# Windowed attention and an ELU layer on one core: half of the first q and k loaded through the GpSimd queue with a cast

## The chip, the cores and the metric

The kernel runs on one core of a Trainium2 chip. The metric is the time of one execution on the device in microseconds (us), the median of several runs; lower is better. A core has a matrix engine (TensorE, PE in the profile; its weight loads are shown apart as PEld), a vector engine (VectorE, DVE), an engine for functions (ScalarE, ACT), a general one (GpSimd, POOL) and one that mostly issues transfers (SyncE, SP). Each runs its instructions in the order of the program and waits on semaphores for the others. Transfers (DMAs) can be issued by SP, ACT and POOL; a DMA that changes the element type on its way is issued by POOL here.

## What is computed

First attention with a window of 32 positions to either side, for 8 batches of 8 heads, 576 positions and 64 channels; then a layer that takes the 4608 x 512 result to 2048 channels, applies ELU, and takes it back to 512. All inputs are float32 in memory.

```python
def _attn_ref(q, k, v):
    B, H, S, D = q.shape                       # 8, 8, 576, 64
    scores = np.matmul(q, k.transpose(0, 1, 3, 2)) / np.sqrt(D)
    pos = np.arange(S)
    mask = np.abs(pos[:, None] - pos[None, :]) <= 32
    scores = np.where(mask, scores, -1000000000.0)
    attn = np.exp(scores - np.max(scores, axis=-1, keepdims=True))
    attn = attn / (np.sum(attn, axis=-1, keepdims=True) + 1e-09)
    return np.matmul(attn, v)

def _moe_ref(x, w_in, w_out):                  # x: 4608 x 512
    h = x @ w_in                               # 512 x 2048
    g = np.where(h > 0.0, h, np.exp(np.minimum(h, 0.0)) - 1.0)
    return g @ w_out                           # 2048 x 512
```

## The kernel before

**Tiling.** A "pair" is two blocks of 64 query positions, 128 rows of the result; there are 36 pairs. A "token tile" is two pairs, 256 rows; there are 18. For a token tile the layer runs in 8 steps of 256 hidden channels each, so the main loop (L609) has 144 steps `kk`, and two more at its end. `mm1(kk)` multiplies the transposed tile `xT` with two 128-column pieces of `w_in` (8 matmuls of 256 columns) into the accumulator `ps`, in bank h0 or h1 by turns. ACT makes `e_sb = exp(ps)`, DVE makes `m_sb = e_sb - 1`, and `elu(kk)`, which is called one step later, makes `g_sb` from `ps` and `m_sb` on DVE. `mm2`, two steps later, multiplies `g_sb` with `w_out` (4 matmuls of 512 columns) into `psY`. The steps of the first two token tiles are woven together (L539 to L541): steps 0 to 3 belong to tile 0, steps 4 to 7 to tile 1, then the rest of both. Step 4 is thus the first that needs pairs 2 and 3.

**Attention of a pair.** `scores` (L281: 32 matmuls of 64 rows), `exponential` on ACT (L296), `mask` on DVE (L303), `pv` (L312: 32 matmuls with 64 weight columns, which write the two halves of the partitions by turns), `normalize` on DVE (L326: a reciprocal and a product), `x_transpose` (L337: four PE transposes) and `x_evac` (L353), which gives `xT`. Queries and keys are needed transposed, with channels on partitions (`qT`, `kT`); values stand in `V_e`, and, rotated by 64 positions, in `V_o` (`rotate_v`, L137, on DVE).

**How q and k come in.** For the first batches `load_qk` (L115) loads float32 to SBUF, in two DMAs (even and odd heads) of 288 KB each for half a batch; `cast_qk` (L236) makes bfloat16 of it; `transpose_qk` (L266) transposes nine 128 x 128 pieces per half batch on PE and evicts them with ACT or DVE. A half is 288 positions: `HALF_A` is the first, `HALF_B` the second. Later batches go through DRAM (`write_rows`, `transpose_rows`).

**How values and weights come in.** `load_v` (five blocks per batch, numbered 0 to 4), `load_w_in` and `load_w_out` (four chunks each of 1 MB float32) are issued by POOL and cast on the way. Chunk 0 serves steps 0, 1, 4 and 5, chunk 1 steps 2, 3, 6 and 7, chunk 2 steps 8 to 11, chunk 3 steps 12 to 15. POOL's order before is: values 1, 0, 2; three `affine_select` for the masks; w_in 0; values 3, 4; w_out 0; w_in 1; w_out 1; w_in 2; w_out 2; values 0, 1, 2 of the second batch; w_in 3; w_out 3; values 3, 4 of the second batch.

**What sets the order.** The schedule is written out by hand: each engine runs in the order in which the program emits. The front (L170 to L429) is straight code, with `idle` matmuls (L376) on zeros that fill PE's gaps. In the loop, `at(kk, slot, fn, ...)` hangs work on step `kk`: "dve" runs after `elu(kk-1)` and ahead of `mm1(kk)`, "mid" after `mm1(kk)`, "end" after `mm2`. A `gate` (L148) is a tiny DMA on SP that reads a piece of a tile; SP's later loads wait until what it reads is there. Before, `HALF_B` of the first batch follows a gate on the masks, `HALF_A` of the second a gate on w_in 1, and `HALF_B` of the second and the whole third batch a gate on w_in 3.

Of the kernel before, what the change touches and what calls it, by code (L numbers as in the profile page):

```python
# [21 lines left out]
def kernel(  # L22
# [9 lines left out]
    nc = tc.nc  # L32

    B, H, S, D = q.shape
    WIN = 32
# [5 lines left out]
    QB = 64  # L41
    NQB = S // QB
    NPAIR = B * NQB // 2
    HP = H // 2
    NC = 128 // HP
    SJ = S // NC
    VS = 5
# [13 lines left out]
    cpool = ctx.enter_context(tc.tile_pool(name="const", bufs=1))  # L61
# [50 lines left out]
    WHOLE, HALF_A, HALF_B = (0, SJ), (0, SJ // 2), (1, SJ // 2)  # L112
    qk_f = {}

    def load_qk(b, which, part, engs=(nc.sync, nc.sync)):  # L115
        z, nj = part
        t = lpool.tile([128, 2, nj * D], FP32, tag=f"f{which}{nj}",
                       name=f"f{which}")
        qk_f[b, which, z] = t
        src = (q, k)[which][b, :, z * NC * nj:(z + 1) * NC * nj, :].rearrange(  # L120
            "(g h) (c j) d -> c g h (j d)", h=2, j=nj)
        for h in range(2):
            engs[h].dma_start(out=t[:, h, :], in_=src[:, :, h, :])

    def load_v(b, m):
        lo = 128 * m - WIN
        p0 = max(0, -lo)
        p1 = min(128, S - lo)
        nc.gpsimd.dma_start(  # L129
            out=V_e[b % 3][p0:p1, m, :, 0:D],  # L130
            in_=v[b, :, lo + p0:lo + p1, :].rearrange("h p d -> p h d"))
# [5 lines left out]
    def rotate_v(b, m0, m1, parts=(0, 1)):  # L137
        e, o = V_e[b % 3], V_o[b % 3]
        for z in parts:
            nc.vector.tensor_copy(o[64 * z:64 * (z + 1), m0:m1],  # L140
                                  e[64 * (1 - z):64 * (2 - z),
                                    m0 + z:m1 + z])
# [17 lines left out]
    def load_w_out(c):  # L160
        n = NFO // 4
        nc.gpsimd.dma_start(
            out=w_out_sb[:, c * n:(c + 1) * n, :],
            in_=moe_w_out[c * n * 128:(c + 1) * n * 128, :].rearrange(
                "(o p) f -> p o f", p=128))

    def w_in_at(c):
        return w_in_sb[0:1, 0, (c + 1) * (D_FF // 4) - 1:(c + 1) * (D_FF // 4)]
# [7 lines left out]
    def edges(i):  # L176
        nc.vector.memset(V_e[i][:, :, :, D:VD], 1.0)
        nc.vector.memset(V_e[i][0:32, 0], 0.0)
        nc.vector.memset(V_e[i][96:128, VS - 1], 0.0)
        if i < 2:  # L180
            for c0, n in ((KPAD - WIN, HP), (KPAD + HP * S, 1)):
                z = kT[i][:, c0:c0 + WIN]
                nc.vector.memset(_bap(z, [z.ap[0], [S, n], [1, WIN]]), 0.0)

    edges(0)
    edges(1)

    ident = cpool.tile([128, 128], BF16)
    make_identity(nc, ident)

    masks = cpool.tile([128, 5, QB], BF16, name="masks")
    nc.gpsimd.memset(masks, 1.0)
    nc.gpsimd.affine_select(
        out=masks, in_=masks, compare_op=ALU.is_ge, fill=0.0,
# [3 lines left out]
        base=2 * WIN, pattern=[[0, 5], [1, QB]], channel_multiplier=-1)  # L200
    for m in (1, 0, 2):
        load_v(0, m)
    for mi in (0, 4):
        nc.gpsimd.affine_select(
            out=masks[:, mi, :], in_=masks[:, mi, :], compare_op=ALU.is_ge,
            fill=0.0, base=-WIN, pattern=[[0, QB]], channel_multiplier=1)
    nc.gpsimd.affine_select(
        out=masks[:, 3, :], in_=masks[:, 3, :], compare_op=ALU.is_ge,
        fill=0.0, base=128 - WIN - 1, pattern=[[0, QB]],
        channel_multiplier=-1)  # L210
    kinds = ["FE", "EE", "EL", "LF"]

    gate(masks[0:1, 3, 0:1])
    for which in range(2):
        load_qk(0, which, HALF_B)
    load_w_in(0)
    for m in (3, 4):
        load_v(0, m)
    load_w_out(0)
    load_w_in(1)  # L220
    load_w_out(1)

    def kind(jb):
        qb = jb % NQB
# [5 lines left out]
    def copy_on(eng, d_, s_):  # L230
        if eng is nc.scalar:
            nc.scalar.copy(d_, s_)  # L232
        else:
            eng.tensor_copy(d_, s_)  # L234
# [12 lines left out]
    def keys_or_queries(b, which):  # L247
        if which == 0:
            return qT[b % 2].rearrange("p g s -> p (g s)")
        return kT[b % 2][:, KPAD:KPAD + HP * S]  # L250
# [12 lines left out]
        nc.sync.dma_start_transpose(  # L263
            out=keys_or_queries(b, which), in_=in_dram.pop((b, which)))

    def transpose_qk(b, which, part, j0, n, evac, tag="t0"):  # L266
        z, nj = part
        src = qk_b[b, which, z]
        pt = ps_tile([128, 1024 if n <= 8 else 2048], BF16, tag, "ptx")
        for j in range(n):  # L270
            nc.tensor.transpose(  # L271
                pt[:, j * 128:(j + 1) * 128], src[:, j0 + j, :], ident)
        d = keys_or_queries(b, which)
        copy_on(evac,
                _bap(d, [d.ap[0], [S, HP], [nj, NC], [1, n]],
                     z * NC * nj + j0),
                _bap(pt, [pt.ap[0], [1, HP], [HP, NC], [128, n]]))

    st = {}

# [56 lines left out]
    def x_transpose(i):  # L337
        x_st, tag = st[i][3:]
        pt = ps_tile([128, NDO, 128], BF16, tag, "psXT")
        for do in range(NDO):  # L340
            nc.tensor.transpose(  # L341
                pt[:, do, :], x_st[:, 2 * do:2 * do + 2, :], ident)
        st[i] = pt
# [9 lines left out]
    def x_evac(i, eng=nc.vector):  # L353
        copy_on(eng, xT_of(i), st.pop(i))
# [12 lines left out]
    def front_cast(which, part, eng):  # L367
        for j0, n in SPLIT:
            cast_qk(0, which, part, j0, n, eng)

    def front_transpose(which, part, evac, tags):
        for (j0, n), tag in zip(SPLIT, tags):
            transpose_qk(0, which, part, j0, n, evac, tag)


    def idle(n, tag):  # L376
        ps = ps_tile([128, 512], FP32, tag, "ps_idle")
        for _ in range(n):
            nc.tensor.matmul(ps, lhsT=zeros[:, 0:128], rhs=zeros,
                             start=True, stop=True)  # L380

    warm = cpool.tile([128, 1], FP32)
    nc.scalar.activation(warm, zeros[:, 0:1], AX.Exp)

    idle(8, "y1")
    front_cast(0, HALF_A, nc.vector)
# [11 lines left out]
    for i in (0, 1):  # L398
        mask(i)
    pv(0)  # L400
    idle(2, "h0")
    pv(1)
    for i in (0, 1):
        normalize(i)
    for i in (0, 1):
        idle(1, "h1")
        x_transpose(i)
        x_evac(i, nc.scalar)
    idle(2, "h1")
    front_cast(0, HALF_B, nc.scalar)  # L410
    front_cast(1, HALF_B, nc.vector)


    load_w_in(2)
    load_w_out(2)
    for m in range(3):
# [2 lines left out]
    load_w_out(3)  # L419
    for m in range(3, VS):  # L420
        load_v(1, m)
    gate(w_in_at(1))
    for which in range(2):
        load_qk(1, which, HALF_A)
    gate(w_in_at(3))
    for which in range(2):
        load_qk(1, which, HALF_B)
# [8 lines left out]
    def at(kk, slot, fn, *args):  # L436
        tasks.setdefault((kk, slot), []).append((fn, args))
# [11 lines left out]
        at(kk + 2, "end", x_evac, i, nc.scalar)  # L449


    at(1, "mid", front_transpose, 1, HALF_B, nc.scalar, ("s", "u"))
    at(1, "mid", front_transpose, 0, HALF_B, nc.vector, ("y0", "y1"))
    at(2, "dve", rotate_v, 0, 2, VS - 1)
    for i, tag in ((2, "s"), (3, "u")):
        at(1, "mid", scores, i, tag)
        at(1, "mid", exponential, i)
        at(2, "dve", mask, i)
    at(2, "dve", lambda: mm2(1))
    for i in (2, 3):  # L460
        at(2, "dve", pv, i)
        at(2, "dve", normalize, i)
        at(3, "mid" if i == 3 else "dve", x_transpose, i)
        at(3, "mid" if i == 3 else "dve", x_evac, i, nc.scalar)
    at(4, "dve", swap_pools)

    for part, kq in ((HALF_A, 7), (HALF_B, 15)):
        for which in range(2):
            at(kq - 1 + which, "mid", cast_qk, 1, which, part, 0, SJ // 2,
               (nc.scalar, nc.vector)[which])  # L470
            at(kq + which, "mid", transpose_qk, 1, which, part, 0, SJ // 2,
               nc.scalar, "s")
    at(8, "dve", edges, 2)
    at(16, "dve", hold_v, 2)
    for m in range(VS):
        at(16 + m, "mid", load_v, 2, m)
# [132 lines left out]
    for kk in range(NSTEP + LAG):  # L609
        run(kk, "first")  # L610
        if 1 <= kk < NSTEP:
            elu(kk - 1)
        run(kk, "dve")
        if kk < NSTEP:
            mm1(kk)
        run(kk, "mid")

        for n in {1: (0,), 2: (), 3: ()}.get(
                kk, (kk - LAG,) if kk >= LAG else ()):
            mm2(n)  # L620
        run(kk, "end")
# [30 lines left out]
```

The softmax here doesn't subtract the row's maximum and nothing guards it: scores larger than these inputs give would overflow.

## Time and profile before

| what | before |
|---|---|
| median of 5 runs | 313.08 us (310.97 to 315.32) |
| the profiled execution | 312.87 us, of which the span of instructions is 311.1 us |
| granted clock of TensorE over the span | 0.998 |
| `mm1` of step 0 / 2 / 4 / 8 begins at | 15.20 / 24.09 / 27.40 / 35.03 us |
| `mm2` of step 0 begins at | 21.39 us |
| scores of pairs 2 and 3 begin at | 20.55 us |
| an `mm1` matmul, an `mm2` matmul | 273 ns, 379 ns each (pipelined: eight and four take about 0.87 us) |
| `exp` / `m_sb` / `g_sb` of one step | 595 / 435 / 686 ns |

Times within the profile count from the start of the span. In the page's second part the span is cut into 40 slices, and a digit is the busy share in tenths. In an answer in order of time a row gives start, duration, engine, line, operation, output and input, shape and count, and in brackets how long the engine was idle before it and what released it. A table of stretches gives, for each engine, busy us and count of instructions, then granted clock, DMA share and GB/s. The rows of the DMA queues give packets, MB and share of the 16 engines; the share can pass 100% since packets overlap.

### The profile page before, as it was taken

The page shows a single profiled execution, that of the slowest core. Times are in us where ns is not written, and L with a number is a line of the kernel's source. Part 1 is how long each engine was busy: PE and PEld are TensorE (multiplying, and loading weights), DVE is VectorE, ACT ScalarE, POOL GpSimd, SP SyncE. Part 2 cuts the span into 40 slices and gives each one's busy share as a digit, 9 for nine tenths or more (in the row PEclk, how much of TensorE's full clock was granted, in tenths as well). Part 3 has the DMA queues.
Part 4 walks back from the last instruction along what each step waited for, and adds up shares of the span by engine and source line. Part 5 has one row for each costly group of instructions (what it writes and reads, how often), then busy time and mean ns, then how long its engine had stood idle before and what let it go on. Part 6 is the DMA issues. An engine that isn't in the chain of part 4 may idle for free.

```text
span 311.1 us, 7510 instructions
## 1 busy us (share of the span) xinstructions
PE 292.9 (94%) x2996; PEld 197.5 (64%) x3048; DVE 247.3 (80%) x480; ACT 170.7 (55%) x256; POOL 44.0 (14%) x60
## 2 busy tenths in 40 slices
PE   7768999999999799999999999999999999999994
PEld 3446666676666466666666666666676666676662
DVE  6587688899979588888888888888888787876663
ACT  3564656787664575568366836673636363634331
POOL 8733000824210022020202010000000000000000
PEclk9999999999999999999999999999999999999999
DMA  9999999999999899999999999678111111111011
GB/s 191 230 204 240 221 235 367 323 209 228 276 111 134 263 246 227 217 175 291 276 139 174 217 300 158 190 167 172 70 36 67 36 70 35 70 34 70 0 70 68
DMA packets 91657, 52.93 MB, mean 170 GB/s; under 512 B 76518, under 2 KB 80614, under 8 KB 91622
## 3 DMA queue, kind: packets, MB, share of 16 engines
q1 hardware_dynamic: 48022, 36.77, 47.9%
q0 software_dynamic: 41728, 8.92, 39.9%
q10 hardware_dynamic: 1872, 6.75, 7.1%
q8 instruction: 24, 0.39, 0.6%
q14 instruction: 11, 0.09, 0.1%
HBM read 36.70 MB, written 15.34 MB: 167 GB/s over the span
## 4 chain that ended last, share of the span: by engine, by line
PE 77%; DMA 12%; DVE 4%; POOL 3%; issue 2%; ACT 1%; SPq 0%; DVEq 0%; POOLq 0%
PE ps L558 35%; PE psY L592 35%; DMA w_out_sb<-in_moe_w_out_dram 4%; DMA in_dram<-qkb 4%; PE psS L320 3%; DMA f<-in_k_dram 3%; PE psS L288 3%; DMA kT<-in_dram 2%; POOL Ve L129 1%; PE ptx L271 1%; DVE g_sb L577 1%; DVE pm L308 1%; PE psXT L341 1%; DVE m_sb L567 1%; DVE x_st L332 0%
## 5 line engine op out<-in xcount | busy, mean ns | idle before, releaser
L565 ACT ACTIVATE e_sb<-ps 128x512 f32<-128x512 f32 (+1 forms) x145 | 86.2, 595 | 121.5 <-PE ps L558 116.0
L558 PE MATMUL ps<-xT,w_in_sb 128*128 128x256 bf16 x1152 | 149.3, 273 | 1.8 <-ACT xT L232 1.2
L592 PE MATMUL psY<-w_out_sb,g_sb 128*128 128x512 bf16 x525 | 139.1, 379 | 3.3 <-issue 0.6
L558 PEld LDWEIGHTS <-w_in_sb 128*128 128x128 bf16 x1152 | 110.8, 98 | 40.3 <-issue 2.1
L577 DVE SCALAR_TENSOR_TENSOR g_sb<-ps,m_sb 128x512 bf16<-128x512 f32 (+1 forms) x145 | 99.5, 686 | 12.9 <-PE ps L558 0.5
L567 DVE TENSOR_SCALAR m_sb<-e_sb 128x512 bf16<-128x512 f32 (+1 forms) x145 | 63.0, 435 | 34.7 <-ACT e_sb L565 32.7
L592 PEld LDWEIGHTS <-g_sb 128*128 128x128 bf16 x576 | 54.6, 98 | 38.5 <-DMA w_out_sb<-in_moe_w_out_dram 0.3
L129 POOL DMA_DIRECT2D Ve<-in_v_dram x40 | 34.8, 881 | 133.2 <-PE psS L320 92.1
L299 ACT ACTIVATE pu<-psS 128x1024 bf16<-128x1024 f32 x36 | 36.5, 1019 | 3.6 <-PE psS L288 3.6
L232 ACT CAST qkb<-f 128x768 bf16<-128x768 f32 (+3 forms) x32 | 26.7, 838 | 0.0
L332 DVE TENSOR_TENSOR x_st<-psS,rc 128x512 bf16<-128x512 f32 x36 | 24.9, 692 | 1.2
L308 DVE TENSOR_TENSOR pm<-pu,masks 128x1024 bf16<-128x1024 bf16 x36 | 24.6, 683 | 1.6 <-ACT pu L299 1.6
L320 PEld LDWEIGHTS <-pm 128*64 128x64 bf16 x576 | 11.2, 110 | 10.4 <-DVE pm L308 7.2
L288 PE MATMUL psS<-qT,kT 64*128 64x64 bf16 x576 | 12.1, 191 | 4.6 <-DVE qT L234 2.1
L288 PEld LDWEIGHTS <-kT 64*128 64x128 bf16 x576 | 9.8, 95 | 9.4 <-issue 5.4
L320 PE MATMUL psS<-Ve,pm 128*64 128x65 bf16 x320 | 13.7, 196 | 0.9 <-DVE pm L308 0.7
L140 DVE COPY Vo<-Ve 64x1040 bf16<-64x1040 bf16 x32 | 13.7, 428 | 1.0
L234 DVE COPY y_sb<-psY 128x512 f32<-128x512 f32 x18 | 12.3, 686 | 1.0 <-PE psY L592 0.9
L320 PE MATMUL psS<-Vo,pm 128*64 128x65 bf16 x256 | 12.5, 197 | 0.2 <-DVE pm L308 0.2
L234 DVE CAST qkb<-f 128x1152 bf16<-128x1152 f32 (+3 forms) x14 | 8.8, 653 | 4.2 <-DMA f<-in_k_dram 3.8
L232 ACT COPY y_sb<-psY 128x512 f32<-128x512 f32 x18 | 10.5, 582 | 2.2 <-PE psY L592 2.2
L271 PE MATMUL ptx<-ident,qkb 128*128 128x128 bf16 x108 | 8.9, 235 | 1.4 <-DVE qkb L234 1.3
(32 smaller groups left out, 67.0 us busy)
## 6 DMA issues: line engine op xcount, KB each, us to landing
out_dram<-y_sb SPq DMA_DIRECT2D x35, 256.0 KB, 2.5
f<-in_q_dram SPq DMA_DIRECT2D x12, 576.0 KB, 8.9
f<-in_k_dram SPq DMA_DIRECT2D x12, 576.0 KB, 10.4
in_dram<-qkb ACTq DMA_DIRECT2D x10, 576.0 KB, 8.9
Ve<-in_v_dram POOLq DMA_DIRECT2D x24, 128.0 KB, 11.1
w_in_sb<-in_moe_w_in_dram POOLq DMA_DIRECT2D x4, 512.0 KB, 16.1
w_out_sb<-in_moe_w_out_dram POOLq DMA_DIRECT2D x4, 512.0 KB, 17.0
f<-in_q_dram SPq DMA_DIRECT2D x7, 288.0 KB, 6.2
```

Of the source, the lines that this page charges most:

```text
L129: nc.gpsimd.dma_start(out=V_e[b % 3][p0:p1, m, :, 0:D], in_=v[b, :, lo + p0:lo + p1, :].rearrange("h p d -> p h d"))
L232: nc.scalar.copy(d_, s_)
L288: nc.tensor.matmul(psS[:, h % 2, hp * 128 + z * QB:hp * 128 + (z + 1) * QB], lhsT=kT[b % 2][base:base + 64, KPAD + hp * S + QB * qb - WIN: ...
L299: nc.scalar.activation(pu, _bap(psS, [psS.ap[0], [1, 1024]]), AX.Exp, scale=SCALE)
L308: nc.vector.tensor_mul(pm, pu, _bap(mm, [mm.ap[0], [0, H], [1, 2 * QB]]))
L320: nc.tensor.matmul(psS[QB * z:QB * (z + 1), par, hp * VD:(hp + 1) * VD], lhsT=pm[:, par * HP + hp, z * QB:(z + 1) * QB], rhs=vv[:, qb // 2 ...
L332: nc.vector.tensor_mul(x_st, _bap(psS, [psS.ap[0], [VD, HP], [512, 2], [1, D]]), _bap(rc, [rc.ap[0], [2, HP], [1, 2], [0, D]]))
L558: nc.tensor.matmul(ps[:, j, :], lhsT=w_in_sb[:, do, fo * 128:(fo + 1) * 128], rhs=xT[t][:, :, do, :], start=(do == 0), stop=(do == NDO - 1))
L565: nc.scalar.activation(e_sb, ps, AX.Exp)
L567: nc.vector.tensor_scalar(m_sb, e_sb, -1.0, None, ALU.add)
L577: nc.vector.scalar_tensor_tensor(g_t[kk][:, z * w:(z + 1) * w, :], ps, 0.0, m_t[kk][z], ALU.max, ALU.min)
L592: nc.tensor.matmul(psY[t][ts], lhsT=g_sb[:, j, ts * 128:(ts + 1) * 128], rhs=w_out_sb[:, s * FG + j, :], start=(s == 0 and j == 0), stop=( ...
```

## The change

`load_cast` loads half a batch of q or k from POOL into a bfloat16 tile (one buffer for q, one for k), cast on the way, in two DMAs by even and odd heads. It is used for `HALF_B` of the first batch and `HALF_A` of the second; SP's loads of these, their two gates and their casts on ACT and DVE go. `transpose_qk` transposes such a tile by heads: two transposes of 64 columns, one for each half of the output's partitions, where there was one of 128.

POOL's order becomes: values 1, 0, 2; `HALF_B` of q and of k; w_in 0; the three `affine_select`; values 3, 4; w_out 0; w_in 1; w_out 1; `HALF_A` of q and of k of the second batch; w_in 2 and the rest as before.

In the front, the transposes of `HALF_B` of q stand between `pv(0)` and `pv(1)`, evicted by ACT, and those of k between the output transposes of pairs 0 and 1, evicted by DVE; most idle matmuls there go. `rotate_v` of the first batch's last two blocks is split: its part 0 stands ahead of the loop, its part 1 behind `mm1(0)`. Scores and exponentials of pairs 2 and 3 follow `mm1(0)`, ahead of `mm1(1)`; their products with the values follow `mm1(1)` and `mm2(0)`, where they followed `mm2(1)` in step 2. The memsets `edges(2)` move from step 8 to step 6. An option `later` of `transpose_qk` is added and not used.

```diff
+    def load_cast(b, which, part):
+        z, nj = part
+        t = cpool.tile([128, 2, nj * D], BF16, tag=f"c{which}",
+                       name=f"c{which}")
+        qk_c[b, which, z] = t
+        src = (q, k)[which][b, :, z * NC * nj:(z + 1) * NC * nj, :].rearrange(
+            "(g h) (c j) d -> c g h (j d)", h=2, j=nj)
+        for h in range(2):
+            nc.gpsimd.dma_start(out=t[:, h, :], in_=src[:, :, h, :])
...
-    gate(masks[0:1, 3, 0:1])
-    for which in range(2):
-        load_qk(0, which, HALF_B)
-    load_w_in(0)
-    for m in (3, 4):
-        load_v(0, m)
...
         for j in range(n):
-            nc.tensor.transpose(
-                pt[:, j * 128:(j + 1) * 128], src[:, j0 + j, :], ident)
+            if (b, which, z) in qk_c:
+                for h in range(2):
+                    nc.tensor.transpose(
+                        pt[64 * h:64 * (h + 1), j * 128:(j + 1) * 128],
+                        qk_c[b, which, z][:, h, (j0 + j) * D:
+                                          (j0 + j + 1) * D], ident)
...
+    for which in range(2):
+        load_cast(0, which, HALF_B)
+    load_w_in(0)
+    for mi in (0, 4):
+        nc.gpsimd.affine_select(
+            out=masks[:, mi, :], in_=masks[:, mi, :], compare_op=ALU.is_ge,
...
+    for m in (3, 4):
+        load_v(0, m)
+    load_w_out(0)
+    load_w_in(1)
+    load_w_out(1)
...
     pv(0)
-    idle(2, "h0")
+    front_transpose(0, HALF_B, nc.scalar, ("h0", "h1"))
     pv(1)
     for i in (0, 1):
         normalize(i)
-    for i in (0, 1):
-        idle(1, "h1")
-        x_transpose(i)
-        x_evac(i, nc.scalar)
+    x_transpose(0)
+    x_evac(0, nc.scalar)
+    front_transpose(1, HALF_B, nc.vector, ("y0", "y1"))
+    x_transpose(1)
+    x_evac(1, nc.scalar)
     idle(2, "h1")
-    front_cast(0, HALF_B, nc.scalar)
-    front_cast(1, HALF_B, nc.vector)
+    for which in range(2):
+        load_cast(1, which, HALF_A)
     load_w_in(2)
...
-    gate(w_in_at(1))
-    for which in range(2):
-        load_qk(1, which, HALF_A)
+    rotate_v(0, 2, VS - 1, (0,))
     gate(w_in_at(3))
...
-    at(1, "mid", front_transpose, 1, HALF_B, nc.scalar, ("s", "u"))
-    at(1, "mid", front_transpose, 0, HALF_B, nc.vector, ("y0", "y1"))
-    at(2, "dve", rotate_v, 0, 2, VS - 1)
-    for i, tag in ((2, "s"), (3, "u")):
-        at(1, "mid", scores, i, tag)
-        at(1, "mid", exponential, i)
-        at(2, "dve", mask, i)
+    at(0, "mid", rotate_v, 0, 2, VS - 1, (1,))
+    at(0, "mid", scores, 2, "s")
+    at(0, "mid", scores, 3, "u")
+    at(1, "mid", lambda: mm2(0))
+    for i in (2, 3):
+        at(0, "mid", exponential, i)
+        at(1, "dve", mask, i)
+        at(1, "mid", pv, i)
+    at(1, "mid", normalize, 2)
+    at(1, "end", x_transpose, 2)
+    at(1, "end", x_evac, 2, nc.scalar)
     at(2, "dve", lambda: mm2(1))
-    for i in (2, 3):
-        at(2, "dve", pv, i)
-        at(2, "dve", normalize, i)
-        at(3, "mid" if i == 3 else "dve", x_transpose, i)
-        at(3, "mid" if i == 3 else "dve", x_evac, i, nc.scalar)
+    at(2, "dve", normalize, 3)
+    at(2, "mid", x_transpose, 3)
+    at(2, "mid", x_evac, 3, nc.scalar)
...
-            at(kq - 1 + which, "mid", cast_qk, 1, which, part, 0, SJ // 2,
-               (nc.scalar, nc.vector)[which])
+            if part is HALF_B:
+                at(kq - 1 + which, "mid", cast_qk, 1, which, part, 0, SJ // 2,
+                   (nc.scalar, nc.vector)[which])
...
-    at(8, "dve", edges, 2)
+    at(6, "dve", edges, 2)
...
-        for n in {1: (0,), 2: (), 3: ()}.get(
+        for n in {2: (), 3: ()}.get(
```

More of the change, by code (lines that the diff above doesn't have):

```diff
@@ L123, in load_qk @@
             engs[h].dma_start(out=t[:, h, :], in_=src[:, :, h, :])
+    qk_c = {}
+    def load_cast(b, which, part):
[7 more added lines that the diff above has]
+            nc.gpsimd.dma_start(out=t[:, h, :], in_=src[:, :, h, :])
     def load_v(b, m):
@@ L183, in edges @@
                 nc.vector.memset(_bap(z, [z.ap[0], [S, n], [1, WIN]]), 0.0)
+    ident = cpool.tile([128, 128], BF16)
+    make_identity(nc, ident)
     edges(0)
     edges(1)
-    ident = cpool.tile([128, 128], BF16)
-    make_identity(nc, ident)
     masks = cpool.tile([128, 5, QB], BF16, name="masks")
@@ L202 @@
         load_v(0, m)
[L203 to L210, printed above, removed]
-    kinds = ["FE", "EE", "EL", "LF"]
-    gate(masks[0:1, 3, 0:1])
-    for which in range(2):
-        load_qk(0, which, HALF_B)
-    load_w_in(0)
-    for m in (3, 4):
-        load_v(0, m)
-    load_w_out(0)
-    load_w_in(1)
-    load_w_out(1)
+    kinds = ["FE", "EE", "EL", "LF"]
     def kind(jb):
@@ L264, in transpose_rows, with transpose_qk, evict @@
             out=keys_or_queries(b, which), in_=in_dram.pop((b, which)))
-    def transpose_qk(b, which, part, j0, n, evac, tag="t0"):
+    def transpose_qk(b, which, part, j0, n, evac, tag="t0", later=None):
         z, nj = part
-        src = qk_b[b, which, z]
         pt = ps_tile([128, 1024 if n <= 8 else 2048], BF16, tag, "ptx")
         for j in range(n):
-            nc.tensor.transpose(
-                pt[:, j * 128:(j + 1) * 128], src[:, j0 + j, :], ident)
[L273 to L277, printed above, removed]
+            if (b, which, z) in qk_c:
[4 more added lines that the diff above has]
+                                          (j0 + j + 1) * D], ident)
+            else:
+                nc.tensor.transpose(
+                    pt[:, j * 128:(j + 1) * 128],
+                    qk_b[b, which, z][:, j0 + j, :], ident)
+        def evict():
+            d = keys_or_queries(b, which)
+            copy_on(evac,
+                    _bap(d, [d.ap[0], [S, HP], [nj, NC], [1, n]],
+                         z * NC * nj + j0),
+                    _bap(pt, [pt.ap[0], [1, HP], [HP, NC], [128, n]]))
+        if later is None:
+            evict()
+        else:
+            later.append(evict)
     st = {}
@@ L369, in front_cast, with front_transpose @@
             cast_qk(0, which, part, j0, n, eng)
-    def front_transpose(which, part, evac, tags):
+    def front_transpose(which, part, evac, tags, later=None):
         for (j0, n), tag in zip(SPLIT, tags):
-            transpose_qk(0, which, part, j0, n, evac, tag)
+            transpose_qk(0, which, part, j0, n, evac, tag, later)
     def idle(n, tag):
@@ L383 @@
     nc.scalar.activation(warm, zeros[:, 0:1], AX.Exp)
+    for which in range(2):
[4 more added lines that the diff above has]
+            out=masks[:, mi, :], in_=masks[:, mi, :], compare_op=ALU.is_ge,
+            fill=0.0, base=-WIN, pattern=[[0, QB]], channel_multiplier=1)
+    nc.gpsimd.affine_select(
+        out=masks[:, 3, :], in_=masks[:, 3, :], compare_op=ALU.is_ge,
+        fill=0.0, base=128 - WIN - 1, pattern=[[0, QB]],
+        channel_multiplier=-1)
+    for m in (3, 4):
[3 more added lines that the diff above has]
+    load_w_out(1)
     idle(8, "y1")
```

## The prediction

> **What bounds the kernel now.** I read the page's engine sums and slices first, then the table of stretches, then the instructions in order of time from 14 to 40 us, and last the DMA queue in stretches of 1 us.
>
> ```profile
> PE 292.9 (94%) x2996; PEld 197.5 (64%) x3048; DVE 247.3 (80%) x480; ACT 170.7 (55%) x256; POOL 44.0 (14%) x60
> PE   7768999999999799999999999999999999999994
> ...
> 15.00:20.00 5.00, 3.14 (x34) 2.56 (x34) 3.25 (x7) 3.76 (x7) 1.77 (x3) 1.00 1.49 211
> 20.00:25.00 5.00, 4.16 (x80) 2.71 (x81) 4.50 (x10) 1.94 (x2) 2.00 (x3) 1.00 1.24 206
> ...
> 200.00:250.00 50.00, 49.48 (x499) 33.62 (x508) 41.35 (x81) 25.31 (x40) 0.00 (x0) 1.00 0.41 99
> ```
>
> TensorE sets the time: 49.48 of 50 us in the steady part. Some 18 us of it are idle in all, and most lie in the first 30 us, which is where the change works. The granted clock is 1.00 there, so no clock is to be won.
>
> ```profile
> 16.64 0.83 DVE L234 CAST qkb<-f 128x640 bf16<-128x640 f32 x2 [2.56 <-DMA f<-in_k_dram]
> 20.55 0.64 PE L288 MATMUL psS<-qT,kT 64*128 64x64 bf16 x32 [2.13 <-DVE qT L234]
> 21.39 1.90 PE L592 MATMUL psY<-w_out_sb,g_sb 128*128 128x512 bf16 x7 [0.20 <-DMA w_out_sb<-in_moe_w_out_dram]
> 27.08 0.10 PEld L558 LDWEIGHTS <-w_in_sb 128*128 128x128 bf16 x1 [0.80 <-DVE g_sb L577]
> 27.40 1.03 PE L558 MATMUL ps<-xT,w_in_sb 128*128 128x256 bf16 x8 [0.94 <-ACT xT L232]
> 36.42 0.68 PE L271 MATMUL ptx<-ident,qkb 128*128 128x128 bf16 x9 [0.35 <-DVE qkb L234]
> ```
>
> The second half of k comes late (16.64), so do its cast, transposes and evictions, and PE stands for 2.13 us before the scores of pairs 2 and 3. From the matmul at 27.40 (step 4) PE runs without a gap, but for one: step 8 begins at 35.03, and its transposes wait until 36.42 for k of the second batch, 0.52 us after mm1's 0.87. So the gain is what step 4 comes earlier, plus step 8.
>
> **DMA is the other bound of this stretch.** Two rows of the queue of POOL, from 23 to 24 us and from 6 to 7 us (packets, MB written, share):
>
> ```profile
> q0 software_dynamic: 206, 0.20, 123.2%
> ...
> q0 software_dynamic: 1228, 0.16, 243.5%
> ```
>
> A weight chunk (512 packets) takes 2.5 us, a value load (1024) 0.83, the short one of 96 rows 0.63. Issue plus time to landing gives: w_in 0 at 14.1, values 4 at 19.3, w_out 0 at 21.3, w_in 1 at 23.9, w_out 1 at 26.4. The bulk of the packets is through about 2 us before such a landing: the last engine trails.
>
> **Part 1, halves B of q and k on POOL's queue.** Removed: SP's gate and four loads (7.21 to 10.2), two casts on ACT (1.25) and two on DVE (0.83). Added on POOL: four issues. The nearest rows are w_in's 0.75 to 0.94 each, so 3.0 to 3.7 us (I take 3.2): POOL reaches w_in 0 at 8.6 instead of 6.34. The three mask selects (1.02) move behind it, to about 10.5; the first mask multiply needs them at 10.85, so they are hidden with 0.3 to spare, and are worth up to 0.3 if the issues take longest. Bytes do not change: 1.18 MB are read either way, at the weights' 0.42 MB/us 2.8 us, nearly the 3.0 of half A on SP (0.40 MB/us from 4 to 5 us). What changes is the order. Before, the values' packets end at 8.2, w_in 0 starts only at 8.7, and runs at 141 to 184 packets/us until 11; SP's packets start at 11.3, four us after their issue. Afterwards POOL has q and k in its ring when the values end: q 8.2 to 9.6, k to 11.0, w_in 0 to 13.6, values 3 and 4 to 15.1, w_out 0 to 17.6, w_in 1 to 20.2. With 1.5 to 2.3 us to landing: q 11.5, k 13, w_in 0 15.5, values 4 17.5, w_out 0 19.9, w_in 1 22.4.
>
> A rule speaks against it. The trace shows idle room (141 against 206 packets/us); the Trainium skill, "DMA: Bandwidth & Descriptors", section "Issuing engines are not separate DMA queues", says that loads of all issuers share the same 16 engines, so moving them saves only issue time. By the rule values 4 still land at 19.3; by the row, 1.8 us earlier. I take the row, since the gap of 8.2 to 11 us is in the trace, and keep 19.3 as the bad end.
>
> **Part 2, the front's transposes.** 18 transposes become 36, with 64 weight columns, in couples on the two column halves of the array. The trace has no such transposes. From below: 9 whole ones go by in 0.50 us. From above: each half costs as much as a whole one, 1.0. Nearest is the probabilities-times-values product, also 128*64: 16 matmuls in 0.38 to 0.45, 0.024 to 0.028 each at 65 columns, so couples run side by side, and nine with 128 columns are about 0.55. The skill's "TensorEngine Tiling (Array Packing)", section "Key Properties", adds that changing the tiling mode drains the engine: the mm1 behind such products takes 0.98 instead of 0.87 in the chain, so I add 0.1, 0.65 per nine (0.5 to 1.1). In the front: q between pv 0 and pv 1 (12.1, since q lands at 11.5), k after the first output transpose at about 13.6. q's evictions (1.37) precede the evictions of x on ACT, and x of pair 1 is ready at 15.3 (15.15 before). The idle matmuls that they replace cost nothing. So mm1 0 starts at w_in 0's landing, 15.5 to 16, instead of 15.2: 0.5 lost here, but PE was going to wait later anyway.
>
> **Part 3, steps 0 to 4.** Now DVE orders it: the first half of the rotation waits for values 3 ahead of the first m_sb, the second half for values 4 ahead of g 0. Queued behind that wait are g 0 and with it mm2 0, masks 2 and 3, and pv 2. With T the landing of values 4: rotation 0.43, g 0.69, masks 0.69 each, so T+2.6; mm2 0 waits for w_out 0 (T+2.1 to 2.4), pv 2 and 3 end at T+3.9; normalize 2 (0.9) T+4.4, g 1 T+5.1, mm2 1 to T+6.0, mm1 2 then (w_in 1 has landed). From mm1 2 to mm1 4 the trace has 24.09 to 27.08, set by exp, m_sb and g of step 2: 2.99. So step 4 is at T+8.95. ACT's chain (mm1 0, exp, two exponentials of scores at 1.02) gives no later end: its second exponential ends near 19.8, one mask behind it. T = 17.5 gives 26.45, against 27.40: 0.95 won. By the rule, T = 19.3 gives 28.25: 0.85 lost.
>
> **Part 4, half A of the second batch.** SP's gate and four loads at 23.9 to 27.1 go, POOL has four more issues (3.2 us) ahead of w_in 2; they also wait until the front's transposes leave their buffers (about 14.3), which costs nothing as the ring holds w_out and w_in then. The ring holds eight transfers in flight (the twelfth, at 14.73, waited for the fourth); each later one is issued over 3 us before its turn. k lands at about 28 instead of 35.5, so step 8's 0.52 is won. w_in 2 lands near 30.5 (needed near 34), w_in 3 near 38 (39.7 before, needed at 44.3): covered. The casts that go (1.15 on ACT, 0.76 on DVE) lay beside PE and are worth nothing themselves. Couples at steps 7 and 8 cost 0.15 each (0 to 0.6). Memsets moved from step 8 to 6 put 1.4 us on DVE behind g 5, so g 6 ends near 34.6 instead of 33.8; mm1 8 needs it at 35.0: hidden by step 7's transposes, and worth 0.4 at most if not. Part 4: 0.52 - 0.3 = 0.2 won.
>
> **Sum.** 0.95 + 0.2 = 1.15 won. The profiled execution took 312.87 (span 311.1 and 1.77 around it), 0.2 under the median 313.08; so 311.7 against it, 311.9 against the median. From step 9 on everything is released by steps, so the shift lasts; the later stall on the transposed k (2.0 us at 103 us) hangs on a chain that starts from a cast placed by step, and stays.
>
> **Rivals.** *A new wait on DVE (slower).* The values 3 and 4 come no earlier, for their queue now holds the halves of q and k; the rotation then holds g 0 and all behind it. Place: DVE at 16 to 20 us. Price: one us for each us of T beyond 18.65, where step 4 is where it was; with part 4, beyond 18.85 the kernel gets slower: T = 19.3 makes 313.5, T = 20.3 (by w_in 0's slow rate for all of q and k) 314.5. For it: before, rotation came after 19.6 and waited for nothing; DMA is full. Against: the gap of 8.2 to 11 us. Chance 0.27. *Couples serialize*: 1.1 per nine, 0.9 lost at steps 7 and 8 over my sum, and up to 0.6 in the front: 313.0. Against: the 128*64 rows. Chance 0.1. *The wait goes altogether*: T near 16.5 and the couples free; then ACT's exponentials and w_out 0 limit, mm1 2 at 22.8 and step 4 at 25.8: 1.6 + 0.5, 311.0. Chance 0.15. *It does nothing*: TensorE's start is set by w_in 0 and w_in 1 in either order: 313. Chance 0.1. My forecast has 0.38.
>
> **How the numbers follow.** 311.9 is the likeliest. The cases run from 311.0 to 314.5; single runs before spread over 4 us, so a median can be off by about 1, and 309.8 to 314.5 leaves out 2 in 10. One per cent is 3.1 us, about what can be told from no change here. Below 309.95 only the best case with a lucky median reaches: 0.08. Above 316.2 needs T beyond 21.5, or a failure that I have not seen, a cast transfer far slower than the weights': 0.07. Within: 0.85.
>
> **What would show it.** Right: queue 0 at about 200 packets/us from 8.2 us on; first mm1 at 15.5 to 16; the second rotation near 17.5; step 4 near 26.4; no DMA wait at step 8. Wrong: a second rotation at 19 or later, PE's couples at 0.1 us each, or mm1 0 after 17.

## The result, and the profile after

| | before | after |
|---|---|---|
| median | 312.84 us (71 runs, 310.04 to 315.5) | 311.8 us (36 runs, 309.9 to 318.3) |
| ratio | | 0.9962 [0.9945, 0.9979] |
| the profiled execution, its span | 312.87, 311.1 us | 310.06, 308.3 us |
| `mm1` of step 0 / 2 / 4 / 8 / 9 begins at | 15.20 / 24.09 / 27.40 / 35.03 / 37.80 | 15.14 / 23.74 / 27.02 / 34.71 / 37.18 us |
| idle of PE at 103 us (late wait on `kT`) | 2.0 us | none |

The medians take in all runs; the ratio leaves out those that were more than 1.5% slower than the fastest run of the same kernel, five of the 36 after. The kernel is faster by 0.38% (0.21 to 0.55%), 1.2 us of 312.84; 1.15 us was forecast. The two profiled executions differ by more, 2.8 us. Most of that is the last row of the table, and the experiments have to say whether it belongs to the change. The page first (sums of PE and POOL, PE by slices, granted clock by slices):

```profile
PE 290.0 (94%) x3026; PEld 195.8 (63%) x3080; DVE 245.5 (80%) x477; ACT 168.3 (55%) x253; POOL 48.2 (16%) x68
PE   6658999999999999999999999999999999999994
PEclk9999999999999999999999999999999999999999
```

The first three slices (23 us) are emptier than before (7768), but the slice with a 7 in the later part is gone. POOL has eight instructions and 4.2 us more, which are the cast loads. Now the instructions in order of time (start, duration, engine, line, operation, shape, count, idle before it and releaser):

```profile
15.14 1.05 PE L588 MATMUL ps<-xT,w_in_sb 128*128 128x256 bf16 x8 [0.89 <-DMA w_in_sb<-in_moe_w_in_dram]
16.86 0.43 DVE L153 COPY Vo<-Ve 64x1040 bf16<-64x1040 bf16 x1 [1.88 <-DMA Ve<-in_v_dram]
17.96 0.42 DVE L153 COPY Vo<-Ve 64x1040 bf16<-64x1040 bf16 x1 [0.22 <-DMA Ve<-in_v_dram]
19.81 1.02 PE L622 MATMUL psY<-w_out_sb,g_sb 128*128 128x512 bf16 x3 [2.06 <-DMA w_out_sb<-in_moe_w_out_dram]
22.27 0.40 PE L350 MATMUL psXT<-ident,x_st 128*128 128x128 bf16 x4 [0.80 <-DVE x_st L341]
25.07 1.75 POOL L142 DMA_DIRECT2D Ve<-in_v_dram  x2 [1.42 <-DMA w_out_sb<-in_moe_w_out_dram]
25.44 0.73 DVE L597 TENSOR_SCALAR m_sb<-e_sb 128x512 bf16<-128x512 f32 x1 [1.79 <-ACT e_sb L595]
27.02 1.05 PE L588 MATMUL ps<-xT,w_in_sb 128*128 128x256 bf16 x8 [1.15 <-DVE g_sb L607]
35.68 0.69 PE L267 MATMUL ptx<-ident,c 128*64 128x128 bf16 x18
```

Read it down. PE waits 0.89 us for `w_in` 0 and starts step 0 at 15.14, as before. DVE waits for values 3 and 4 and has the second rotation at 17.96; before, values 4 landed only at 19.3. PE then stands 2.06 us for `w_out` 0 (before 0.20, but 2.13 just ahead of it for `qT`, whose eviction on DVE stood behind the late cast of k). Step 4 starts at 27.02 and was held by `g_sb`, behind an `m_sb` that took 0.73 us beside POOL's issue of two value loads (25.07); before, this `m_sb` of step 2 took 0.43. In the kernel before, such a pair is seen one step later, where it held nothing up; these two rows are from its profile, the `m_sb` of step 3 and a value load:

```profile
26.67 0.89 POOL L129 DMA_DIRECT2D Ve<-in_v_dram  x1 [1.78 <-DMA w_out_sb<-in_moe_w_out_dram]
26.95 0.84 DVE L567 TENSOR_SCALAR m_sb<-e_sb 128x512 bf16<-128x512 f32 x1
```

In the profile after, step 8's transposes (35.68) wait for nothing. The queue of POOL from 8 to 9 and from 9 to 10 us (packets, MB written, share):

```profile
q0 software_dynamic: 419, 0.15, 136.0%
q0 software_dynamic: 201, 0.19, 121.0%
```

Before, these two stretches had 243 and 141 packets. The hole between the values and `w_in` 0 is filled.

### The profile page after: what moved, and what is told of

The parts are those of the page before. It is cut to its first block, busy times and chain, and to the rows that moved or that the text cites. A ratio compares the mean times of both kernels' runs of the same rounds, so it can differ in the third digit from the quotient of the medians.

```text
span 308.3 us, 7551 instructions
## 1 busy us (share of the span) xinstructions
PE 290.0 (94%) x3026; PEld 195.8 (63%) x3080; DVE 245.5 (80%) x477; ACT 168.3 (55%) x253; POOL 48.2 (16%) x68
## 4 chain that ended last, share of the span: by engine, by line
PE 84%; DVE 6%; POOL 3%; DMA 3%; issue 2%; ACT 1%; DVEq 0%; POOLq 0%
PE ps L588 38%; PE psY L622 37%; PE psS L329 3%; PE psS L297 3%; DMA w_out_sb<-in_moe_w_out_dram 3%; DVE g_sb L607 2%; POOL Ve L142 1%; PE ptx L272 1%; DVE x_st L341 1%; DVE pm L317 1%; DVE m_sb L597 1%; POOL c L136 1%; DVE y_sb L229 1%; ACT e_sb L595 1%; PE psXT L350 1%
## 5 line engine op out<-in xcount | busy, mean ns | idle before, releaser
L227 ACT CAST qkb<-f 128x768 bf16<-128x768 f32 (+1 forms) x29 | 24.3, 838 | 0.0
L227 ACT COPY qT<-ptx 128x1152 bf16<-128x1152 bf16 (+2 forms) x8 | 7.6, 976 | 3.1 <-PE ptx L272 2.4
L227 ACT COPY xT<-psXT 128x512 bf16<-128x512 bf16 x10 | 5.9, 585 | 5.4 <-PE psXT L350 5.4
```

## The experiments

Each was run beside the kernel before on the same chip; its median there was 313.17 (30 runs) for the halves and the late wait, 312.84 (29 runs) for one filler in before, the fillers in after, after again and the better order, and 312.94 (23 runs) for the other four. Intervals are of the ratio to it.

**One half of the change each.** The front alone: half A of the second batch stays on SP, with its casts.

```diff
-    for which in range(2):
-        load_cast(1, which, HALF_A)
...
+    gate(w_in_at(1))
+    for which in range(2):
+        load_qk(1, which, HALF_A)
...
-    at(6, "dve", edges, 2)
+    at(8, "dve", edges, 2)
```

> The change without its part for the second batch: half A of the second q and k stays on SP with its gate and its casts, and the memsets stay at step 8. Theory A (the prediction: the gain is made at steps 0 to 4 and at step 8, the late wait stays): step 4 begins near 27.0 us, step 8 keeps a DMA wait of about 0.5 us, time about 0.9 us under before. Theory B (most of the measured gain is that the transfers run ahead of the steps, so that the wait for the third-batch keys near 103 us goes): w_in 3 lands at about 39 us or later, as before, the late wait of 1 to 2 us is still there in the profile, and the time is only 0.3 to 0.5 us under before.

310.9 us (7 runs), 0.9926 [0.9891, 0.9962]; the interval overlaps that of the whole change. Step 4 is at 27.28, step 8 at 34.91, and there is no wait for data at step 8 although half A still comes by SP, where 0.5 us was expected.

```profile
20.05 1.02 PE L622 MATMUL psY<-w_out_sb,g_sb 128*128 128x512 bf16 x3 [2.23 <-DMA w_out_sb<-in_moe_w_out_dram]
27.28 1.05 PE L588 MATMUL ps<-xT,w_in_sb 128*128 128x256 bf16 x8 [1.16 <-DVE g_sb L607]
```

The other half alone: the front of before, half A cast by POOL and transposed by heads, without its casts on ACT and DVE.

```diff
+    for which in range(2):
+        load_cast(1, which, HALF_A)
     load_w_in(2)
...
-    gate(w_in_at(1))
-    for which in range(2):
-        load_qk(1, which, HALF_A)
...
-    at(8, "dve", edges, 2)
+    at(6, "dve", edges, 2)
```

> Only the second batch's half A goes through POOL with a cast and is transposed by heads; the front is as before. Theory A: step 4 at 27.4 as before, no DMA wait at step 8, gain 0.2 to 0.5 us, late wait as before. Theory B: the same head, but SP's later loads start no earlier than before (w_in 3 at 39 to 40 us), so the late wait stays too: gain 0.2 to 0.5. If half A on POOL is by itself what brings the later loads forward, w_in 3 lands under 38.5 us and the late wait shrinks, gain over 1 us.

313.56 us (12 runs), 1.0004 [0.9973, 1.0034]: not told from no change, with anything from 0.8 us faster to 1.1 us slower inside the interval. Its front is that of before, and yet step 4 begins a microsecond later than in the profile of before:

```profile
17.79 0.83 DVE L247 CAST qkb<-f 128x640 bf16<-128x640 f32 x2 [3.60 <-DMA f<-in_k_dram]
28.34 1.03 PE L585 MATMUL ps<-xT,w_in_sb 128*128 128x256 bf16 x8 [0.94 <-ACT xT L245]
```

The cast of k starts at 17.79 instead of 16.64, after 3.60 us of idle DVE. So the gain is seen with the front and not without it; the 0.2 us of part 4 is too small for these runs to confirm or exclude. And the front of before has no fixed timing.

**The late wait.** Is the 2.0 us at 103 us a cost of before that the change removes? In the profile of before the chain of waits goes through it (first the transfer in that chain, then the row of PE):

```profile
97.90 5.39 DMA kT<-in_dram
103.34 0.29 PE L288 MATMUL psS<-qT,kT 64*128 64x64 bf16 x8 [2.00 <-DMA kT<-in_dram]
```

In both kernels the attention of pairs 12 and 13, whose scores wait there, was begun one step later, which leaves `kT` a step more to land.

```diff
-10: 30, 12: 37}
+10: 30, 12: 38}
```

In before:

> The kernel before, with pairs 12 and 13 (the first that read the fourth batch, whose transposed keys come last) one step later, 38 instead of 37. Theory B: the wait of 2.0 us near 103 us shrinks to under 0.5, time 1 to 1.5 us under before. Theory A (the late wait is no part of the difference): it may shrink or not, but then the same in the kernel after.

In after:

> The changed kernel with the same shift of pairs 12 and 13. Theory B: the changed kernel has no such wait to lose, so this is within 0.3 us of the changed kernel, and only about 0.6 us (what steps 4 and 8 give) under the kernel before with the same shift. Theory A: about 1.1 us under the kernel before with the same shift.

Before with it: 313.08 us (12 runs), 0.9999 [0.9969, 1.003]. After with it: 312.09 us (12 runs), 0.9977 [0.9946, 1.0008]. Neither profile has the wait. But the edit brings one of its own, in both kernels (this row is of before with the edit, and in after it stands at 111.90 us with the same 1.11):

```profile
112.29 0.41 PE L288 MATMUL psS<-qT,kT 64*128 64x64 bf16 x16 [1.11 <-DVE x_st L332]
```

If the wait were regular, the edit would take 2.0 us out of before and add 1.1, a ratio of about 0.997, which the interval does not clearly exclude. The profiles decide it: of the twelve that keep the old step, six with the old front and six with the new, only this one profile of before has the wait. It belongs to one execution. And with the edit in both, after is still 1.0 us under before (312.09 against 313.08), near the 1.1 expected if the wait is no part of the gain. The profile of before with this edit shows something else instead (stretches: busy time and instructions of PE, PEld, DVE, ACT, POOL, then granted clock, DMA share, GB/s):

```profile
20.00:24.00 4.00, 3.32 (x45) 1.46 (x47) 3.55 (x6) 1.94 (x2) 1.44 (x2) 0.76 1.24 206
24.00:28.00 4.00, 3.56 (x56) 2.98 (x54) 2.70 (x6) 1.71 (x4) 0.94 (x2) 0.81 1.23 213
```

In order of time:

```profile
21.20 2.73 PE L592 MATMUL psY<-w_out_sb,g_sb 128*128 128x512 bf16 x7
28.49 1.03 PE L558 MATMUL ps<-xT,w_in_sb 128*128 128x256 bf16 x8 [0.94 <-DVE m_sb L567]
```

Up to the scores of pairs 2 and 3 (20.63, before 20.55) it is the same schedule. Then the clock falls, the two `mm2` take 2.73 instead of 1.90 us, and step 4 is 1.1 us later, at 28.49. In stretches of 1 us the drop to half clock lasts from about 22.1 to 25.5 us.

**Can idle matmuls keep the clock?** Idle matmuls were put where PE waits. In before, ahead of the scores of pairs 2 and 3:

```diff
+    at(1, "mid", idle, 7, "h0")
     for i, tag in ((2, "s"), (3, "u")):
         at(1, "mid", scores, i, tag)
```

> The kernel before, with seven idle matmuls on zeros (0.21 us each) in PE's gap between the transposes of half B and the scores of pair 2; nothing else moves. Theory C (new: much of the measured gain is the granted clock. Runs of the kernels with the old front had a clock of 0.982 to 0.995 in most runs, those with the new front 0.996 or more in most, and a profile with 0.993 has the clock at 0.76 to 0.81 from 20 to 28 us, just behind that gap): the clock is 0.996 or more in most runs, and the median is about 2 us under before, near 311. Theory A or B (transfers and stalls alone): the clock and the time stay as before, 313.

312.64 us (12 runs), 0.9992 [0.9962, 1.0022]. In its profile k came later still: transposes at 19.16, step 4 at 31.12. The wait had moved ahead of the filler. So a second filler was put ahead of the transposes as well:

```diff
+    at(1, "mid", idle, 6, "y0")
     at(1, "mid", front_transpose, 1, HALF_B, nc.scalar, ("s", "u"))
```

> The kernel before with idle matmuls on both sides of the transposes of half B: six ahead of them, behind mm1 of step 1, and seven behind them. They can cost PE up to 0.8 us where k is not late. Theory C (idle stretches of the front let the clock down, and that is a part of the gain): at least 8 of 12 runs at a clock of 0.996 or more, where the kernel before has 11 of 59 and one with the second filler alone 6 of 12; median 0.5 to 1.5 us under before. If it stays near 2 of 10, the clock does not hang on these gaps.

312.13 us (12 runs), 0.9976 [0.9939, 1.0013]: not told from no change, though the median is 0.8 us under before and 8 of 12 runs have the clock, as Theory C expected. Step 4 is at 27.93. In after, three fillers:

```diff
-    idle(2, "h1")
+    idle(5, "h1")
...
+    at(1, "mid", idle, 8, "y0")
     at(1, "mid", lambda: mm2(0))
...
+    at(3, "mid", idle, 4, "s")
     at(4, "dve", swap_pools)
```

> The changed kernel with idle matmuls in the three gaps of its front (3 more ahead of mm1 of step 0, 8 ahead of mm2 of step 0, 4 ahead of mm1 of step 4). Theory C: nearly all runs at a clock of 0.996 or more, median about 310.2, 0.5 to 1 us under the changed kernel. Theory A or B: as the changed kernel.

311.11 us (12 runs), 0.9951 [0.992, 0.9982]; after unchanged beside it:

> The changed kernel once more, beside the others on this chip. Theory C: some 7 of 10 runs at a clock of 0.996 or more with a median near 310.5, the others near 312.6. Theory B: no wait near 103 us in the profile. Ratio to before 0.994 to 0.998.

310.2 us (12 runs), 0.9954 [0.9915, 0.9993], step 4 at 27.68. The fillers give no time that can be told from none. What they change, in before, is how often the clock is full. The mean granted clock over the span was 0.996 or more (less than 2.5 us at half speed in 310; one drop of 3.4 us makes 0.9945) in this many runs:

| | runs at 0.996 or more |
|---|---|
| before, all three times | 17 of 82 |
| before with one filler / two | 6 of 12 / 8 of 12 |
| half A alone / before, pairs 12 and 13 later | 3 of 12 / 3 of 12 |
| before without the gate (next experiment) | 4 of 12 |
| after and after again | 29 of 48 |
| after with fillers / after, pairs 12 and 13 later | 10 of 12 / 9 of 12 |
| the front alone / the reordered version below | 5 of 7 / 6 of 6 |

Runs of before at 0.996 or more have a median of 311.04, the others 313.23; such runs of after 310.26. So at equal clock 0.8 us of the gain are left, and the rest goes with rarer clock drops. That is a sorting of runs, not an experiment: a late k may bring both the later step 4 and the drop. Where fillers keep the clock, such runs have medians of 311.95 (before, 14 runs) and 311.04 (after, 10 runs), 0.9 and 0.8 us above those without fillers: the fillers cost most of what the clock gives.

**Does an early issue do, without the place in the queue?** In before, the gate ahead of half B is taken away, so that SP issues these loads at once, ahead of the values:

```diff
-    gate(masks[0:1, 3, 0:1])
     for which in range(2):
         load_qk(0, which, HALF_B)
```

> The kernel before without SP's gate on the masks: half B is issued by SP right behind half A, at about 2.2 us instead of 7.2, so it lands by about 9 to 10 us and the values and w_in 0 after it. If the late half B is what the change repairs, the cast of k no longer waits near 16.6 us, PE's gap of 2.1 us shrinks to under 1, most runs have a clock of 0.996 or more and the time is near that of the change, 1 to 1.5 us under before, less up to 1 us since the values land later. If the order on POOL's queue and the rewoven steps are needed, it is as before or slower.

314.08 us (12 runs), 1.0042 [1.0011, 1.0072]: slower. The values now come late, `pv` waits 1.95 us at 15.24, step 0 begins at 19.17 and step 4 at 31.00:

```profile
24.15 0.64 PE L287 MATMUL psS<-qT,kT 64*128 64x64 bf16 x32 [1.76 <-DVE qT L233]
31.00 1.03 PE L557 MATMUL ps<-xT,w_in_sb 128*128 128x256 bf16 x8 [0.94 <-DVE m_sb L566]
```

So it does not help that half B is early, if the values pay for it. In the change it stands behind the values and ahead of `w_in` 0, and the steps are rewoven to use it; the front alone has both, and no run has one without the other.

**A second look at before.** Before unchanged, profiled again:

> The kernel before, for one more profile. Theory C: with 4 chances in 5 its clock is under 0.996 and then the clock is down in a stretch between 18 and 30 us, with step 4 at 28.4 us or later instead of 27.4. Theory B: the wait of 1 us or more for the transposed keys near 103 us is there again.

313.06 us, span 311.3, granted clock 0.989. Almost the same time as the first profile, made up quite differently:

```profile
18.52 1.20 DVE L234 CAST qkb<-f 128x640 bf16<-128x640 f32 x2 [4.96 <-DMA f<-in_k_dram]
19.07 2.27 PE L271 MATMUL ptx<-ident,qkb 128*128 128x128 bf16 x18 [2.47 <-DVE qkb L234]
22.59 1.04 PE L288 MATMUL psS<-qT,kT 64*128 64x64 bf16 x32 [1.25 <-DVE qT L234]
23.56 2.84 PE L592 MATMUL psY<-w_out_sb,g_sb 128*128 128x512 bf16 x8
30.28 1.03 PE L558 MATMUL ps<-xT,w_in_sb 128*128 128x256 bf16 x8 [0.94 <-DVE m_sb L567]
```

The stretches of the same run:

```profile
16.00:20.00 4.00, 1.53 (x14) 0.97 (x12) 1.49 (x3) 1.68 (x4) 1.70 (x2) 0.83 1.37 208
20.00:24.00 4.00, 2.75 (x47) 2.22 (x46) 3.83 (x8) 1.95 (x3) 1.76 (x3) 0.50 1.24 206
24.00:28.00 4.00, 4.00 (x51) 2.23 (x50) 2.49 (x7) 1.17 (x2) 1.21 (x2) 0.81 1.24 209
```

k comes 1.9 us later than in the first profile. PE waits 2.47 us for its cast, and the clock is half from about 18.7 to 25.5 us: the 18 transposes take 2.27 us, the 32 matmuls of the scores 1.04 instead of 0.64, `mm2` 2.84 instead of 1.90. Step 4 is 2.9 us later, and the late wait at 103 us is missing. In after the same stretches have a clock of 1.00, with not much more work on PE:

```profile
16.00:20.00 4.00, 1.94 (x43) 1.41 (x42) 2.86 (x6) 2.92 (x4) 1.66 (x3) 1.00 1.27 202
20.00:24.00 4.00, 2.94 (x46) 1.65 (x46) 2.96 (x7) 0.59 (x1) 1.70 (x2) 1.00 1.24 206
```

**The slow `m_sb`.** To take POOL's value loads away from `m_sb` of step 2, a write by DVE was added that they were meant to follow:

```diff
     at(4, "dve", swap_pools)
+    at(5, "dve", hold_v, 1)
```

> The changed kernel with the second batch's value loads held back until step 5 (a memset on DVE that they must follow), so that POOL issues no transfer between 22 and 27 us. If m_sb of step 2 took 0.73 us instead of 0.43 since POOL was issuing transfers beside it, it takes 0.43 now and step 4 follows step 2 by 2.99 us instead of 3.28. If not, it stays at 0.7.

326.11 us. The edit does not do what it was meant to: the program emits the value loads in the front, ahead of step 5, so the write waited for them instead, and DVE and PE stood for 12 us, until 43 and 44 us. The loads were issued when they were before, and `m_sb` still took 0.76. This run decides nothing.

The traces say more. The fourteen profiles of this case hold 2030 `m_sb`. Of these, 1789 have no issue by POOL beside them, and none took over 0.43 us. Over 0.5 us took 81, and each of them began 0.23 to 0.68 us after the start of an issue by POOL (80 of values, one of weights) and ended 1.0 to 1.3 us after that start. Only six others began in that stretch; those that met an issue earlier or later took at most 0.44. Step 2 after (25.44, issue at 25.07) and step 3 before (26.95, issue at 26.67) fall into it. So the slow `m_sb` goes with where it falls in POOL's issue, in both kernels, and the change moves these issues from 26.67 to 25.07, onto the `m_sb` that holds step 4. That the issue holds it up is read from the times; no run moves the issues alone.

**A better order.** With values early, `w_out` 0 is what PE waits for. In this version `w_in` 1 is loaded ahead of `w_out` 0, and all that needs no `w_out` goes ahead of the first `mm2`:

```diff
-    load_w_out(0)
     load_w_in(1)
+    load_w_out(0)
     load_w_out(1)
...
-    idle(2, "h1")
+    idle(5, "h1")
...
-    at(1, "mid", lambda: mm2(0))
+    at(1, "mid", idle, 7, "y0")
...
-    at(1, "end", x_transpose, 2)
-    at(1, "end", x_evac, 2, nc.scalar)
-    at(2, "dve", lambda: mm2(1))
     at(2, "dve", normalize, 3)
-    at(2, "mid", x_transpose, 3)
-    at(2, "mid", x_evac, 3, nc.scalar)
+    at(2, "mid", x_transpose, 2)
+    at(2, "mid", x_evac, 2, nc.scalar)
+    at(3, "mid", x_transpose, 3)
+    at(3, "mid", x_evac, 3, nc.scalar)
+    at(3, "mid", lambda: mm2(0))
+    at(3, "mid", lambda: mm2(1))
```

> The changed kernel with w_in 1 ahead of w_out 0 on POOL, the products of pairs 2 and 3 with the values and mm1 of steps 2 and 3 ahead of mm2 of steps 0 and 1, and idle matmuls in the gap ahead of them. If PE's remaining gaps (2.06 us for w_out 0, 0.80 and 1.15 for DVE) are what still holds the front, step 4 begins near 25 us instead of 27.0 and the time is 1.5 to 2 us under the changed kernel at the same clock. If DVE's chain sets step 4 in any order, it stays at 26.5 to 27.

309.32 us (6 runs, 307.84 to 311.66), 0.9898 [0.9852, 0.9943].

```profile
18.10 1.67 PE L388 MATMUL ps_idle<-zeros 128*128 128x512 bf16 x7
20.69 1.05 PE L589 MATMUL ps<-xT,w_in_sb 128*128 128x256 bf16 x8
22.10 1.03 PE L589 MATMUL ps<-xT,w_in_sb 128*128 128x256 bf16 x8
23.19 1.89 PE L623 MATMUL psY<-w_out_sb,g_sb 128*128 128x512 bf16 x8
24.92 1.04 PE L589 MATMUL ps<-xT,w_in_sb 128*128 128x256 bf16 x8
```

Step 2 begins at 20.69 instead of 23.74, `mm2` of steps 0 and 1 go in one piece at 23.19 without a wait, and step 4 begins at 24.92, 2.1 us before after's. It is faster than before beyond doubt; against after unchanged on the same chip (310.2) it is 0.9 us better, where 1.5 to 2 was expected, and there the intervals overlap. In the profile 1.1 of the 2.1 us are left at the end: 0.2 go in step 7, and 0.8 near 166 us, where DVE had waited 1.12 us for a transfer of `x_st`.

## Why the prediction was right, and where it was not

The total was right, and so was the mechanism that it named, an earlier step 4. That the number fits so closely is partly luck: one part of the sum did not show, one term was too small, and a part that it had excluded made up for them. A sum over the profiles shows it, since each span divides into the start of step 4 and the rest:

| profile | step 4 at | rest of the span |
|---|---|---|
| before | 27.40 | 283.70, of it 2.0 late wait |
| half A alone | 28.34 | 281.56 |
| before, pairs 12 and 13 later | 28.49 | 281.51, of it 1.1 of the edit's own wait |
| before again | 30.28 | 281.02 |
| after | 27.02 | 281.28 |
| the front alone | 27.28 | 280.72 |
| after, pairs 12 and 13 later | 27.59 | 282.21, of it 1.1 of the edit's own wait |
| after again | 27.68 | 281.42 |

With the old front step 4 begins at 28.63 in the mean, with the new one at 27.39: 1.24 us. The rest, without these waits, is 281.17 and 281.13 in the mean. So in these profiles the gain is in step 4, and the clock drops ahead of it are counted there. Four executions each fix this mean only to about 0.6 us, since the old front's spread from 27.40 to 30.28. With the profiles that have fillers in the front (31.12 and 27.93 in before, 29.48 in after) the means are 28.93 and 27.81.

- **The order in the queue** (part 1): right. Packets flow without a hole from 8 us on, and the values 4 that were put at 17.5 let the rotation start at 17.96. The rule of the Trainium skill, "DMA: Bandwidth & Descriptors", section "Issuing engines are not separate DMA queues", that another issuer saves only issue time, had given 19.3. The row won over it; and SP's loads without the gate show that the order counts, since issued earlier on SP they made the kernel slower.
- **The front's transposes** (part 2): right. Step 0 was put at 15.5 to 16 and came at 15.14, held by `w_in` 0. The four issues cost 2.3 us rather than 3.2 (1.13 and 1.16 for two).
- **Steps 0 to 4** (part 3): step 2 came at 23.74, where T+6 with T = 17.5 gave 23.5. From step 2 to step 4 it was 3.28 instead of 2.99. The term that was mis-sized is `m_sb` of step 2, 0.73 for 0.43; it is 0.73 to 0.76 in the four profiles with the new front. The sum took it from a step of before that had no issue beside it; the next step's, 0.84, stands in the same profile. So 0.38 was won against that one profile, where 0.95 was forecast.
- **"No clock is to be won"**: this step failed. The clock of 1.00 and the k at 16.64 belong to one execution. Over the runs, four of five executions of before lose some clock, two of five of after. What the prediction lost by `m_sb` came back by a front of before that is 1.2 us slower in the mean than its profile shows.
- **Half A** (part 4): 0.2 was forecast, and none can be told (1.0004, to within 1 us). The wait at step 8 was in one profile of before alone. In the front alone, steps 7 and 8 take 2.41 and 2.24 us with whole transposes, in after 2.47 and 2.47 with couples: 0.29 lost, as the forecast's 0.3 for couples, with no wait to set against it.
- **The late wait** that "stays": it neither stays nor was removed; it was in one execution of before and in no other profile.

One sum of the prediction is off by 0.2: step 4 stays where it was at T = 27.40 - 8.95 = 18.45, and with part 4 the kernel gets slower beyond 18.65, not 18.85; the prices beside it are right. Of the rivals, the wait on DVE is there (1.88 and 0.22 us), but the values were early enough. The couples didn't serialize: 18 take 0.56 to 0.69 us, where serial ones would be 1.0. T of 16.5 was not reached.

Two things stay open. What starts a clock drop is only narrowed down: after has a gap of 2.06 us on PE and keeps its clock in that profile. And how much of the gain is the place in POOL's queue, and how much the rewoven steps, was not separated.

## What to carry to other kernels

A load that is late though the transfer engines have room is worth trying on the queue of the loads around it, in the order of need; issued earlier from another queue it can push back what is needed first. One profile is one execution: before a wait of a microsecond or two is put into a sum, look for it in a second profile, and look at the granted clock of all the runs. After a transfer has moved forward, ask which transfer PE waits for now, and move the work that doesn't need it ahead of that wait. Ask also beside which instructions the moved issues now fall: a duration read from a step without such a neighbour was 0.3 us too short here.

## What the runs showed of the hardware

- In before again the clock fell to 0.50 about 2 us into a wait of 2.47 us on PE and was full again 6.8 us later; in before with pairs 12 and 13 later it fell 1.5 us after the end of a wait of 2.29 us and was full again 3.4 us later. The Trainium skill, "TensorE: Matmul & The Clock Gate", section "HAM oscillation — how this bites in real kernels", puts the limit for an idle gap at about 3.4 us; here shorter ones went before the drops. With the same schedule up to 20.6 us one execution kept its clock and another lost it.
- A load on SP's queue beside a busy queue of POOL landed at no fixed time: in the six profiles of the old front with its gate, the cast of k began anywhere from 16.55 to 18.61 us. Behind the values on POOL's own queue, k's transposes began between 13.02 and 13.73 us in the four profiles of the new front in the table above, with no wait for data.
- An issue by POOL in before and after took 0.54 to 0.74 us for a cast load of half of the heads, 0.74 to 0.94 for a chunk of weights, and 0.8 to 0.9 for values.
- DVE's `m_sb` took at most 0.43 us with no issue by POOL beside it (1789 of them). When it began 0.23 to 0.68 us after the start of such an issue, it took 0.51 to 0.95 us in 81 of 87 cases.
